# Reordering the second tile's attention, interleaving the first groups of the first product, and splitting the last rows of a fused attention and feed-forward kernel

## The chip, the cores, the metric

One core of one Trainium2 chip. The metric is the device time of one execution in microseconds (us). A program on one core has no second die to compare with, so a run counts as slow when it is over 1.5% above the fastest of its kernel; every run told of here is of the state fast. Ratios are the mean time of one kernel's fast runs over the mean of the other's fast runs of the same rounds, so they are not quite the ratio of the medians that I quote beside them.

## The reference, cut to what matters

```python
def _attn_ref(q, k, v):              # (8, 8, 576, 64) each; nine chunks of 64 rows
    scores = scale * np.matmul(q_c, k_c.transpose(0, 1, 2, 4, 3))
    scores = scores - np.max(scores, axis=-1, keepdims=True)
    attn = np.exp(scores)
    attn = attn / (np.sum(attn, axis=-1, keepdims=True) + 1e-09)
    return np.matmul(attn, v_c)      # back to (8, 8, 576, 64)

def _moe_ref(x, w_in, w_out):        # (4608, 512), (512, 2048), (2048, 512)
    h = x @ w_in
    g = 0.5 * h * (1.0 + erf(h * inv_sqrt2))
    return g @ w_out
```

## The kernel before

The 4608 tokens are cut into nine tiles of 512. A tile goes through attention (four pairs of heads, `g`), a first product `mm1` (16 groups of four matmuls, each followed by a GELU on ACT) and a second product `mm2` (16 slots of four matmuls). The attention of tile t+1 is placed between the slots of tile t's second product. The first two tiles differ from the later ones: weights are still arriving and being cast, and q and k are transposed on PE instead of by the transfers.

Names in what follows: PE multiplies matrices, ACT is ScalarE, DVE VectorE, POOL GpSimd, and SP (SyncE) issues transfers. In the attention the scores go into `s_ps`, their exponentials into `pT`, the sums of these into `sums_ps`, the reciprocals, spread over the tile, into `rc` (by way of `rb`), the product with v into `av_ps`, and the result is `x`. To evacuate is to copy a finished result out of PSUM, so that its buffer comes free.

```python
    def att_sums(t):

        sum_ps = ps_at.tile([P, MT], f32, tag="at", name="sums_ps")
        for g in range(G):
            nc.tensor.matmul(sum_ps[QD * g:QD * (g + 1)], ones_c[:], tiles[t]["pT", g][:], start=True, stop=True,
                             tile_position=(0, QD * g))
        t1 = work.tile([P, NB, 32], f32, tag="t1", name="t1", bufs=2)
        nc.vector.transpose(t1[:], sum_ps[:].rearrange("p (n e) -> p n e", e=32))
        r1 = work.tile([P, 2, NB], f32, tag="r1", name="r1", bufs=2)
        nc.vector.reciprocal(r1[:], t1[:].rearrange("p n (r e) -> p r n e", r=2)[:, :, :, 0])
        rb = work.tile([P, G, NB], f32, tag="rb", name="rb", bufs=2)
        for g in range(G):
            for s in range(G):
                nc.scalar.copy(rb[QD * s:QD * (s + 1), g], r1[QD * g:QD * (g + 1), s // 2])
        tiles[t]["rb"] = rb

    def att_rc(t, g):

        rb = tiles[t]["rb"]
        rc = work.tile([P, NB, 32], f32, tag="rc", name="rc", bufs=4)
        nc.vector.transpose(rc[:], rb[:, g].to_broadcast([P, NB, 32]))
        tiles[t]["rc", g] = rc
...
    def att_av(t, g):
        st = tiles[t]
        av_ps = ps_at.tile([P, CT, CH], f32, tag="at", name="av_ps")
        for i in range(CT):
            nc.tensor.matmul(av_ps[:, i, :], v_bds[t % NV][:, i, g, :], st["pT", g][:, i, :], start=True, stop=True)
        nc.vector.tensor_tensor(
            st["x"][:, g, :], av_ps[:].rearrange("p i e -> p (i e)"),
            st["rc", g][:].rearrange("p n e -> p (n e)"), op=mybir.AluOpType.mult)

    NB = MT // 32
    DV, AC, PO = nc.vector.tensor_copy, nc.scalar.copy, nc.gpsimd.tensor_copy

    def att_units(t, cq=DV, ck=DV):
        tiles[t]["x"] = xpool.tile([P, G, MT], bf16, tag="x", name="x")
        T = []
        for g in range(G):
            T += [lambda g=g: att_Tq(t, g, cq), lambda g=g: att_Tk(t, g, ck)]
        S_ = [lambda g=g: att_S(t, g) for g in range(G)]
        if t > 1:
            T = [lambda g=g: flip_k(t, g, ck) for g in range(G)]
            S_ = [lambda g=g: att_S_flipped(t, g) for g in range(G)]
            U = [lambda: att_sums(t), *[lambda g=g: att_rc(t, g) for g in range(G)]]
        else:
            U = [lambda g=g: att_sum(t, g) for g in range(G)]
        A = [lambda g=g: att_av(t, g) for g in range(G)]
        return T, S_, U, A


    def mm1_slot(t, f):
        st = tiles[t]
        if f == 0:
            st["h"] = hpool.tile([P, FF, MT], bf16, tag="h", name="h")
        h_ps = ps_mm.tile([P, MT], f32, tag="mm", name="h_ps")
        for ks in range(KS):
            nc.tensor.matmul(h_ps[:], w_in_sb[:, ks, f * P:(f + 1) * P], st["x"][:, ks, :],
                             start=(ks == 0), stop=(ks == KS - 1))
        nc.scalar.activation(st["h"][:, f, :], h_ps[:], Act.Gelu)

    NQ = 4
    def mm2_slot(t, ms, qt):
        st = tiles[t]
        if qt == 0:
            pool, tag = (ps_at, "at") if t == 0 and ms == 3 else (ps_mm, "mm")
            st["y_ps", ms] = pool.tile([P, d_model], f32, tag=tag, name="y_ps")
        y_ps = st["y_ps", ms]
        for f in range(qt * FF // NQ, (qt + 1) * FF // NQ):
            nc.tensor.matmul(y_ps[:], st["h"][:, f, ms * P:(ms + 1) * P], w_out_sb[:, f, :],
                             start=(f == 0), stop=(f == FF - 1))
        if qt == NQ - 1:
            y_sb = ypool.tile([P, d_model], f32, tag="y", name="y_sb")
            (AC if t == 0 or ms % 2 == 0 and t + 1 < NT else DV)(y_sb[:], y_ps[:])
            if t < B:
                m0 = t * S + ms * P
                nc.sync.dma_start(out[m0:m0 + P, :], y_sb[:])
            else:
                for c in range(P // CH):
                    m0 = (ms * (P // CH) + c) * S + MT
                    nc.sync.dma_start(out[m0:m0 + CH, :], y_sb[c * CH:(c + 1) * CH, :])

    def phase(t, extra1, extra2, halved=False):
        nms = MT // P
        if halved:
            order = [(ms, qt) for ms in range(nms) for qt in (0, 1)]
            order += [(ms, qt) for qt in (2, 3) for ms in range(nms)]
        else:
            order = [(ms, qt) for ms in range(nms) for qt in range(NQ)]
        for f in range(FF):
            for u in extra1.get(f, ()):
                u()
            mm1_slot(t, f)
        for s, (ms, qt) in enumerate(order):
            for u in extra2.get(s, ()):
                u()
            mm2_slot(t, ms, qt)
        for u in extra2.get("end", ()):
            u()
...
        for g in range(G):
            cast_v(1, 0, PO, slice(g, g + 1))

        T, S_, U, A = att_units(1, DV, AC)
        def next_qk():
            for nm in "qk":
                load_qk(2, nm)
        phase(0, {}, {5: T[0:2], 6: T[2:4], 7: [*T[4:6], S_[0]], 8: [*T[6:8], S_[1]],
                      9: [U[0], S_[2]], 10: [U[1], next_qk], 11: [S_[3], U[2]],
                      
                      12: [lambda: act_table(Act.Gelu), *[lambda g=g: cast_v(1, 1, AC, slice(g, g + 1)) for g in range(G)]],
                      13: [U[3]], 14: [A[0]], 15: [A[1]], "end": [A[2], A[3]]}, halved=True)
        pool_cast_qk(2)
```

`ps_mm` has three PSUM buffers (h_ps and y_ps share them), `ps_at` three (scores, sums, av; one of them is held by y3 during tile 0's second product), `ps_tp` two.

The softmax here doesn't subtract the row's maximum and nothing guards it: scores larger than these inputs give would overflow.

Of the kernel before, what the change touches and what calls it, by code (L numbers as in the profile page):

```python
# [11 lines left out]
def kernel(  # L12
# [9 lines left out]
    nc = tc.nc  # L22
    P = 128
    f32 = mybir.dt.float32
    bf16 = mybir.dt.bfloat16
    Act = mybir.ActivationFunctionType

    B, H, S, D = q.shape
    CH = 64
# [3 lines left out]
    G = H // 2  # L33
# [99 lines left out]
    def cast_v(t, r, copy, gs=slice(0, G)):  # L133
        sl = slice(CH * r, CH * (r + 1))
        copy(v_bds[t % NV][sl, :, gs, sl].rearrange("p i g d -> p g i d"), tiles[t]["vf"][sl, gs])  # L135
# [9 lines left out]
    def att_Tq(t, g, copy):  # L145
        tp = transposed(t, "q", g)
        qT = work.tile([P, CT, CH], bf16, tag="qT", name="qT", bufs=5)
        copy(qT[:].rearrange("p i (c j) -> p i c j", j=J), tp)
        tiles[t]["qT", g] = qT

    def att_Tk(t, g, copy):
        tp = transposed(t, "k", g)
        for r in range(2):
            sl = slice(CH * r, CH * (r + 1))
            copy(k_bds[g][sl, :, sl].rearrange("p i (c j) -> p i c j", j=J), tp[sl])  # L155
# [16 lines left out]
    def att_S_flipped(t, g):  # L172

        st = tiles[t]
        s_ps = ps_at.tile([P, CT, CH], f32, tag="at", name="s_ps")
        qt = st["qt"][:, g * J:(g + 1) * J].rearrange("p j (i c) -> p i j c", i=CT)
        for i in range(CT):
            nc.tensor.matmul(s_ps[:, i, :].rearrange("p (j c) -> p j c", j=J), k_bds[g][:, i, :], qt[:, i],  # L178
                             start=True, stop=True)
        pT = work.tile([P, CT, CH], bf16, tag="pT", name="pT", bufs=5)  # L180
        nc.scalar.activation(pT[:].rearrange("p i (c j) -> p i c j", j=J),  # L181
                             s_ps[:].rearrange("p i (j c) -> p i c j", j=J), Act.Exp, scale=scale)
        st["pT", g] = pT

    def att_S(t, g):
        st = tiles[t]
        s_ps = ps_at.tile([P, CT, CH], f32, tag="at", name="s_ps")
        for i in range(CT):
            nc.tensor.matmul(s_ps[:, i, :], k_bds[g][:, i, :], st["qT", g][:, i], start=True, stop=True)  # L189
        pT = work.tile([P, CT, CH], bf16, tag="pT", name="pT", bufs=5)  # L190
        nc.scalar.activation(pT[:], s_ps[:], Act.Exp, scale=scale)  # L191
        st["pT", g] = pT
# [34 lines left out]
# [6 lines that stand above are left out]
# [35 lines left out]
    def att_units(t, cq=DV, ck=DV):  # L268
        tiles[t]["x"] = xpool.tile([P, G, MT], bf16, tag="x", name="x")
        T = []  # L270
        for g in range(G):
            T += [lambda g=g: att_Tq(t, g, cq), lambda g=g: att_Tk(t, g, ck)]
        S_ = [lambda g=g: att_S(t, g) for g in range(G)]
        if t > 1:
            T = [lambda g=g: flip_k(t, g, ck) for g in range(G)]
            S_ = [lambda g=g: att_S_flipped(t, g) for g in range(G)]
            U = [lambda: att_sums(t), *[lambda g=g: att_rc(t, g) for g in range(G)]]
        else:
            U = [lambda g=g: att_sum(t, g) for g in range(G)]
        A = [lambda g=g: att_av(t, g) for g in range(G)]  # L280
        return T, S_, U, A


    def mm1_slot(t, f):
        st = tiles[t]
        if f == 0:
            st["h"] = hpool.tile([P, FF, MT], bf16, tag="h", name="h")
        h_ps = ps_mm.tile([P, MT], f32, tag="mm", name="h_ps")
        for ks in range(KS):
            nc.tensor.matmul(h_ps[:], w_in_sb[:, ks, f * P:(f + 1) * P], st["x"][:, ks, :],  # L290
                             start=(ks == 0), stop=(ks == KS - 1))
        nc.scalar.activation(st["h"][:, f, :], h_ps[:], Act.Gelu)  # L292

    NQ = 4
    def mm2_slot(t, ms, qt):
        st = tiles[t]
        if qt == 0:
            pool, tag = (ps_at, "at") if t == 0 and ms == 3 else (ps_mm, "mm")
            st["y_ps", ms] = pool.tile([P, d_model], f32, tag=tag, name="y_ps")
# [12 lines that stand above are left out]
                    m0 = (ms * (P // CH) + c) * S + MT  # L312
                    nc.sync.dma_start(out[m0:m0 + CH, :], y_sb[c * CH:(c + 1) * CH, :])

    def phase(t, extra1, extra2, halved=False):
        nms = MT // P
        if halved:
            order = [(ms, qt) for ms in range(nms) for qt in (0, 1)]
            order += [(ms, qt) for qt in (2, 3) for ms in range(nms)]
        else:  # L320
            order = [(ms, qt) for ms in range(nms) for qt in range(NQ)]
        for f in range(FF):
            for u in extra1.get(f, ()):
                u()
            mm1_slot(t, f)
# [6 lines that stand above are left out]
# [40 lines left out]
    def act_table(func):  # L372
        nc.scalar.activation(act_scratch[:], rest[:, 0:1], func)  # L373

    with tc.manual_schedule():
# [74 lines left out]
                wout[c](i, PO)  # L450
        for g in range(G):
            cast_v(1, 0, PO, slice(g, g + 1))

        T, S_, U, A = att_units(1, DV, AC)
        def next_qk():
            for nm in "qk":
                load_qk(2, nm)
        phase(0, {}, {5: T[0:2], 6: T[2:4], 7: [*T[4:6], S_[0]], 8: [*T[6:8], S_[1]],
                      9: [U[0], S_[2]], 10: [U[1], next_qk], 11: [S_[3], U[2]],
                      
                      12: [lambda: act_table(Act.Gelu), *[lambda g=g: cast_v(1, 1, AC, slice(g, g + 1)) for g in range(G)]],
                      13: [U[3]], 14: [A[0]], 15: [A[1]], "end": [A[2], A[3]]}, halved=True)
        pool_cast_qk(2)
        for t in range(1, NT):
            nxt = t + 1 < NT
# [46 lines left out]
```

## Time and profile before

| | before |
|---|---|
| median of the first three runs | 299.74 us (299.62 to 300.56) |
| span of the profiled run | 297.1 us |
| PE busy | 283.0 us, 95% |
| tile 0's second product | 21.21 us, where 17.8 would do |
| last matmul's end to the end of the span | 5.0 us |

The busy share of PE says that the kernel is near its bound, not where the rest lies. For that one compares stages that do the same work in different tiles, and then asks for the waits inside the stage that is too long. The lines are in the prediction.

### The profile page before, as it was taken

The page shows a single profiled execution, that of the slowest core. Times are in us where ns is not written, and L with a number is a line of the kernel's source. Part 1 is how long each engine was busy: PE and PEld are TensorE (multiplying, and loading weights), DVE is VectorE, ACT ScalarE, POOL GpSimd, SP SyncE. Part 2 cuts the span into 40 slices and gives each one's busy share as a digit, 9 for nine tenths or more (in the row PEclk, how much of TensorE's full clock was granted, in tenths as well). Part 3 has the DMA queues.
Part 4 walks back from the last instruction along what each step waited for, and adds up shares of the span by engine and source line. Part 5 has one row for each costly group of instructions (what it writes and reads, how often), then busy time and mean ns, then how long its engine had stood idle before and what let it go on. Part 6 is the DMA issues. An engine that isn't in the chain of part 4 may idle for free.

```text
span 297.1 us, 4797 instructions
## 1 busy us (share of the span) xinstructions
PE 283.0 (95%) x1820; PEld 138.4 (47%) x1855; DVE 125.4 (42%) x207; ACT 176.1 (59%) x366; POOL 95.3 (32%) x134
## 2 busy tenths in 40 slices
PE   6799988999999999999999999999999999999993
PEld 2554454444544554455445444544454445444441
DVE  6775258441826072517250735163146341630020
ACT  3746377777636863686368637863687368636400
POOL 7869655407620640083006500650002700000000
PEclk9999999999999999999999999999999999999999
DMA  6999999799749814981499149804999850020033
GB/s 225 271 370 407 393 279 305 206 216 308 210 134 283 220 69 131 294 218 54 134 276 238 50 138 291 236 37 135 194 126 149 235 121 2 35 106 2 0 71 71
DMA packets 96198, 53.78 MB, mean 181 GB/s; under 512 B 68528, under 2 KB 87984, under 8 KB 96176
## 3 DMA queue, kind: packets, MB, share of 16 engines
q1 hardware_dynamic: 96176, 53.49, 66.3%
q8 instruction: 14, 0.23, 0.3%
q14 instruction: 8, 0.07, 0.1%
HBM read 36.70 MB, written 9.44 MB: 155 GB/s over the span
## 4 chain that ended last, share of the span: by engine, by line
PE 92%; DVE 3%; ACT 2%; issue 2%; ACTq 0%
PE h_ps L290 41%; PE y_ps L302 41%; PE av_ps L260 3%; PE s_ps L178 2%; ACT k_bd L155 2%; PE tp L142 1%; PE s_ps L189 1%; PE sums_ps L215 1%; PE sum_ps L197 1%; PE rc_ps L248 1%; DVE x L261 1%; DVE t L201 0%; ACT pT L191 0%; DVE q_nat L131 0%; DVE v_bd L73 0%
## 5 line engine op out<-in xcount | busy, mean ns | idle before, releaser
L302 PE MATMUL y_ps<-w_out_sb,h 128*128 128x512 bf16 x554 | 133.6, 379 | 1.1
L290 PE MATMUL h_ps<-x,w_in_sb 128*128 128x512 bf16 x564 | 125.8, 379 | 1.2 <-DVE x L261 0.4
L292 ACT ACTIVATE h<-h_ps 128x512 bf16<-128x512 f32 x144 | 86.0, 597 | 63.5 <-PE h_ps L290 63.5
L290 PEld LDWEIGHTS <-w_in_sb 128*128 128x128 bf16 x576 | 56.1, 98 | 68.8 <-issue 1.7
L302 PEld LDWEIGHTS <-h 128*128 128x128 bf16 x576 | 51.5, 98 | 53.0 <-issue 1.6
L170 DVE COPY k_bd<-k_t 64x512 bf16<-64x512 bf16 x56 | 34.2, 611 | 48.8 <-DMA k_t<-k_nat 47.6
L131 POOL CAST q_nat<-arrival 128x512 bf16<-128x512 f32 x32 | 19.7, 655 | 99.9 <-DMA arrival<-in_q_dram 96.4
L135 POOL CAST v_bd<-arrival 64x2048 bf16<-64x2048 f32 (+1 forms) x26 | 33.8, 1306 | 20.8 <-DMA arrival<-in_v_dram 12.8
L224 ACT COPY rb<-r 32x16 f32<-32x16 f32 x112 | 22.6, 202 | 14.1 <-DVE r L220 12.6
L306 DVE COPY y_sb<-y_ps 128x512 f32<-128x512 f32 x18 | 12.4, 688 | 39.6 <-PE y_ps L302 39.6
L261 DVE TENSOR_TENSOR x<-av_ps,rc 128x512 bf16<-128x512 f32 x36 | 24.5, 689 | 4.0 <-PE av_ps L260 1.1
L218 DVE STREAM_TRANSPOSE t<-sums_ps 128x512 f32<-128x512 f32 x7 | 5.0, 717 | 48.7 <-PE sums_ps L215 48.7
L131 POOL CAST k_nat<-arrival 128x512 bf16<-128x512 f32 x32 | 18.6, 618 | 12.2 <-DMA arrival<-in_k_dram 6.8
L373 ACT ACT_TABLE_LOAD x17 | 21.8, 1283 | 1.0 <-PEq L496 0.7
L231 DVE STREAM_TRANSPOSE rc<-rb 128x512 f32<-128x512 f32 x28 | 19.7, 704 | 6.4 <-ACT rb L224 6.4
L260 PEld LDWEIGHTS <-v_bd 128*128 128x128 bf16 x288 | 13.0, 99 | 7.9 <-issue 0.4
L306 ACT COPY y_sb<-y_ps 128x512 f32<-128x512 f32 x18 | 10.3, 589 | 8.4 <-PE y_ps L302 8.4
L155 ACT COPY k_bd<-tp 64x512 bf16<-64x512 bf16 x16 | 9.3, 579 | 9.3 <-PE tp L142 9.1
L181 ACT ACTIVATE pT<-s_ps 128x512 bf16<-128x512 f32 x28 | 14.7, 592 | 0.0
L260 PE MATMUL av_ps<-pT,v_bd 128*128 128x64 bf16 x288 | 14.3, 194 | 0.1
L178 PEld LDWEIGHTS <-k_bd 128*128 128x128 bf16 x224 | 10.4, 98 | 6.6
L178 PE MATMUL s_ps<-q_t,k_bd 128*128 128x64 bf16 x224 | 11.1, 193 | 0.0
(55 smaller groups left out, 105.7 us busy)
## 6 DMA issues: line engine op xcount, KB each, us to landing
arrival<-in_v_dram SPq DMA_DIRECT2D x72, 128.0 KB, 4.2
out_dram<-y_sb SPq DMA_DIRECT2D x32, 256.0 KB, 2.0
arrival<-in_q_dram SPq DMA_DIRECT2D x7, 1024.0 KB, 6.2
arrival<-in_k_dram SPq DMA_DIRECT2D x7, 1024.0 KB, 8.8
arrival<-in_moe_w_out_dram SPq DMA_DIRECT2D x4, 1024.0 KB, 13.3
arrival<-in_moe_w_in_dram SPq DMA_DIRECT2D x3, 1024.0 KB, 10.5
arrival<-in_q_dram SPq DMA_DIRECT2D x4, 256.0 KB, 4.2
arrival<-in_k_dram SPq DMA_DIRECT2D x4, 256.0 KB, 4.5
```

Source lines behind the costliest of these rows:

```text
L131: copy(st[nm][:, g].rearrange("p j r d -> p r j d"), st[nm + "f"][:, 2 * g:2 * g + 2])
L135: copy(v_bds[t % NV][sl, :, gs, sl].rearrange("p i g d -> p g i d"), tiles[t]["vf"][sl, gs])
L170: copy(k_bds[g][sl, :, sl].rearrange("p i (c j) -> p i c j", j=J), src[sl])
L178: nc.tensor.matmul(s_ps[:, i, :].rearrange("p (j c) -> p j c", j=J), k_bds[g][:, i, :], qt[:, i], start=True, stop=True)
L224: nc.scalar.copy(rb[QD * s:QD * (s + 1), g], r1[QD * g:QD * (g + 1), s // 2])
L260: nc.tensor.matmul(av_ps[:, i, :], v_bds[t % NV][:, i, g, :], st["pT", g][:, i, :], start=True, stop=True)
L261: nc.vector.tensor_tensor(st["x"][:, g, :], av_ps[:].rearrange("p i e -> p (i e)"), st["rc", g][:].rearrange("p n e -> p (n e)"), op=mybir ...
L290: nc.tensor.matmul(h_ps[:], w_in_sb[:, ks, f * P:(f + 1) * P], st["x"][:, ks, :], start=(ks == 0), stop=(ks == KS - 1))
L292: nc.scalar.activation(st["h"][:, f, :], h_ps[:], Act.Gelu)
L302: nc.tensor.matmul(y_ps[:], st["h"][:, f, ms * P:(ms + 1) * P], w_out_sb[:, f, :], start=(f == 0), stop=(f == FF - 1))
L306: (AC if t == 0 or ms % 2 == 0 and t + 1 < NT else DV)(y_sb[:], y_ps[:])
L373: nc.scalar.activation(act_scratch[:], rest[:, 0:1], func)
```

## The change

Its intent: fill PE where tile 1's attention leaves it waiting. q is transposed first and copied by ACT, k's copies are shared between ACT and DVE, the sums of the four head pairs are made by four column-tiled matmuls (each fills a quarter of the rows of one PSUM buffer) as in the later tiles. The first mm1 groups of tiles 0 and 1 run slice by slice of K, so that PE has work while the last x is made. The last 128 rows are cut into two column halves, so that half of the evacuation and transfer lies beside matmuls.

```diff
-        s_ps = ps_at.tile([P, CT, CH], f32, tag="at", name="s_ps")
+        pool, tag = (ps_tp, "tp") if t == 1 and g > 1 else (ps_at, "at")
+        s_ps = pool.tile([P, CT, CH], f32, tag=tag, name="s_ps")
...
-            T += [lambda g=g: att_Tq(t, g, cq), lambda g=g: att_Tk(t, g, ck)]
+            T += [lambda g=g: att_Tq(t, g, cq), lambda g=g: att_Tk(t, g, ck if t == 0 or g % 2 == 0 else DV)]
...
+        if t > 0:
             U = [lambda: att_sums(t), *[lambda g=g: att_rc(t, g) for g in range(G)]]
...
-    def mm1_slot(t, f):
+    def mm1_slot(t, f, n=1):
...
+        h_ps = [ps_mm.tile([P, MT], f32, tag="mm", name="h_ps") for _ in range(n)]
         for ks in range(KS):
+            for a in range(n):
+                nc.tensor.matmul(h_ps[a][:], w_in_sb[:, ks, (f + a) * P:(f + a + 1) * P], st["x"][:, ks, :],
+                                 start=(ks == 0), stop=(ks == KS - 1))
+        for a in range(n):
+            nc.scalar.activation(st["h"][:, f + a, :], h_ps[a][:], Act.Gelu)
...
+    def last_rows(t, ms):
+        h = d_model // 2
+        for a, (pool, tag) in enumerate(((ps_mm, "mm"), (ps_at, "at"))):
...
+            (AC if a == 0 else DV)(y_sb[:], y_ps[:])
+            for c in range(P // CH):
+                m0 = (ms * (P // CH) + c) * S + MT
+                (nc.sync if c == 0 else nc.scalar).dma_start(
+                    out[m0:m0 + CH, a * h:(a + 1) * h], y_sb[c * CH:(c + 1) * CH, :])
...
+        first = (2, 3, 1)[min(t, 2)]
+        mm1_slot(t, 0, first)
+        for f in range(first, FF):
...
+            cast_v(1, 1, PO, slice(g, g + 1))
...
-        T, S_, U, A = att_units(1, DV, AC)
+        T, S_, U, A = att_units(1, AC, AC)
...
+        phase(0, {}, {0: [lambda: act_table(Act.Exp)],
+                      3: [T[0]], 4: [T[2]], 5: [T[4]], 6: [T[6], T[1]], 7: [T[3]], 8: [T[5], S_[0]], 9: [T[7], S_[1], next_qk],
+                      10: [S_[2], S_[3]], 11: [U[0], lambda: act_table(Act.Gelu)], 12: [U[1], A[0]], 13: [U[2], A[1]],
+                      14: [U[3], A[2]], 15: [U[4], A[3]]}, halved=True)
```

Two things are easily overlooked. The second half of tile 1's v casts, `cast_v(1, 1, ...)`, moves from ACT to POOL. And the scores of tile 1's third and fourth pair of heads take their PSUM buffers from `ps_tp`, not from `ps_at`; no run tested that alone.

More of the change, by code (lines that the diff above doesn't have):

```diff
@@ L287, in mm1_slot @@
             st["h"] = hpool.tile([P, FF, MT], bf16, tag="h", name="h")
-        h_ps = ps_mm.tile([P, MT], f32, tag="mm", name="h_ps")
+        h_ps = [ps_mm.tile([P, MT], f32, tag="mm", name="h_ps") for _ in range(n)]
         for ks in range(KS):
-            nc.tensor.matmul(h_ps[:], w_in_sb[:, ks, f * P:(f + 1) * P], st["x"][:, ks, :],
-                             start=(ks == 0), stop=(ks == KS - 1))
-        nc.scalar.activation(st["h"][:, f, :], h_ps[:], Act.Gelu)
+            for a in range(n):
[3 more added lines that the diff above has]
+            nc.scalar.activation(st["h"][:, f + a, :], h_ps[a][:], Act.Gelu)
     NQ = 4
@@ L296, in mm2_slot @@
         st = tiles[t]
+        if t == NT - 1 and ms == MT // P - 1:
+            if qt == 0:
+                last_rows(t, ms)
+            return
         if qt == 0:
@@ L313, in mm2_slot @@
                     nc.sync.dma_start(out[m0:m0 + CH, :], y_sb[c * CH:(c + 1) * CH, :])
+    def last_rows(t, ms):
+        h = d_model // 2
+        for a, (pool, tag) in enumerate(((ps_mm, "mm"), (ps_at, "at"))):
+            y_ps = pool.tile([P, h], f32, tag=tag, name="y_ps")
+            for f in range(FF):
+                nc.tensor.matmul(y_ps[:], tiles[t]["h"][:, f, ms * P:(ms + 1) * P],
+                                 w_out_sb[:, f, a * h:(a + 1) * h], start=(f == 0), stop=(f == FF - 1))
+            y_sb = ypool.tile([P, h], f32, tag="y", name="y_sb")
+            (AC if a == 0 else DV)(y_sb[:], y_ps[:])
[3 more added lines that the diff above has]
+                    out[m0:m0 + CH, a * h:(a + 1) * h], y_sb[c * CH:(c + 1) * CH, :])
     def phase(t, extra1, extra2, halved=False):
@@ L321, in phase @@
             order = [(ms, qt) for ms in range(nms) for qt in range(NQ)]
-        for f in range(FF):
+        first = (2, 3, 1)[min(t, 2)]
+        mm1_slot(t, 0, first)
+        for f in range(first, FF):
             for u in extra1.get(f, ()):
@@ L457, in next_qk @@
                 load_qk(2, nm)
-        phase(0, {}, {5: T[0:2], 6: T[2:4], 7: [*T[4:6], S_[0]], 8: [*T[6:8], S_[1]],
-                      9: [U[0], S_[2]], 10: [U[1], next_qk], 11: [S_[3], U[2]],
-                      12: [lambda: act_table(Act.Gelu), *[lambda g=g: cast_v(1, 1, AC, slice(g, g + 1)) for g in range(G)]],
-                      13: [U[3]], 14: [A[0]], 15: [A[1]], "end": [A[2], A[3]]}, halved=True)
+        phase(0, {}, {0: [lambda: act_table(Act.Exp)],
+                      3: [T[0]], 4: [T[2]], 5: [T[4]], 6: [T[6], T[1]], 7: [T[3]], 8: [T[5], S_[0]], 9: [T[7], S_[1], next_qk],
+                      10: [S_[2], S_[3]], 11: [U[0], lambda: act_table(Act.Gelu)], 12: [U[1], A[0]], 13: [U[2], A[1]],
+                      14: [U[3], A[2]], 15: [U[4], A[3]]}, halved=True)
         pool_cast_qk(2)
```

## The prediction

> **What bounds the kernel now.** I read the page first (busy shares, slices, chain), then the stretches of single stages, then PE's waits, then the order of time around the second tile and the end. From the page:
>
> ```profile
> PE 283.0 (95%) x1820; PEld 138.4 (47%) x1855; DVE 125.4 (42%) x207; ACT 176.1 (59%) x366; POOL 95.3 (32%) x134
> ...
> PE   6799988999999999999999999999999999999993
> ...
> PE 92%; DVE 3%; ACT 2%; issue 2%; ACTq 0%
> ```
>
> PE is full nearly everywhere, and 92% of the chain that ended last is PE's. PE's matmul work is not cut by this change (but for the sums), so all that can be won is PE's idle time: slices 1 and 2 (start), the dip at slices 6 and 7 (37 to 52 us), and the end. To size the dip I compare stages. Columns: the stretch, its length, then busy time of the engines.
>
> ```profile
> 18.50:32.91 14.41, 14.03 (x69) 6.27 (x68) 8.28 (x13) 10.02 (x17) 11.36 (x12) 1.00 1.06 398
> 32.91:54.12 21.21, 19.10 (x162) 10.29 (x164) 11.88 (x23) 13.64 (x23) 11.64 (x22) 1.00 0.90 290
> 54.12:68.60 14.48, 14.09 (x70) 6.24 (x68) 6.05 (x10) 9.80 (x17) 3.02 (x5) 1.00 0.94 230
> 68.60:84.70 16.10, 15.94 (x130) 8.15 (x132) 7.00 (x11) 9.97 (x27) 11.41 (x12) 1.00 0.77 236
> 84.70:98.50 13.80, 13.75 (x64) 6.23 (x64) 5.48 (x9) 8.96 (x15) 1.93 (x4) 1.00 0.92 256
> ```
>
> An undisturbed first product (mm1: 64 matmuls of 512 columns) takes 13.80 us (84.70 on), 0.216 us a matmul. Tile 0's takes 14.41 (0.61 too long), tile 1's 14.48 (0.68 too long). The undisturbed second product with the next tile's attention takes 16.10; the one at 32.91 also has 8 groups of 4 transposes, 0.22 each, so it should take 17.8, and takes 21.21: 3.4 too long. What it waited for (total, times, longest), PE's waits from 30 to 56 us:
>
> ```profile
> PE s_ps L189 <- DVE t L201: 0.8, 1, 0.8
> PE tp L142 <- ACT k_bd L155: 0.7, 2, 0.5
> PE sum_ps L197 <- ACT pT L191: 0.4, 1, 0.4
> PE h_ps L290 <- DVE x L261: 0.2, 1, 0.2
> ```
>
> After 62 us PE waits for nothing at all. So 0.6 + 3.4 + 0.7 = 4.7 us, plus the end, is all there is to win: 1.6% plus a little.
>
> **The Trainium skill.** "TensorE: Matmul & The Clock Gate", Back-to-back issue gap: N/2.4 + 2.5 ns warm, so 216 ns for 512 columns; the trace agrees (13.80/64 = 0.2156). By it 256 columns take 109 ns (an estimate), so cutting 16 matmuls into 32 halves is 3.5 us against 3.45: free, if the extra weight loads hide; here 8 matmuls of 64 columns with their loads take 0.23 us, so they hide. "ScalarE: Activation LUTs", What ACT_TABLE_LOAD costs: 1283 ns plus a drain of 1380 for each switch; here the load is 1.28 us and the next activation follows at once, so I use 1.28 + 0.20. "DMA: Bandwidth & Descriptors", Issuing engines are not separate DMA queues: a second issuing engine saves only the sequencer's time to issue; here an issue is 0.58 us, and at the end two lie one behind the other. Its "Anatomy of one DMA" gives about 2 us fixed; the last output transfers land after 2.2 to 2.4.
>
> **Part 1, tile 0's first two mm1 groups K-slice by K-slice.** Now PE does three matmuls from 18.50 and stands for the last x slice until 19.75 (1.25 us for 0.65 of work). With two groups interleaved it has six (1.29 us) until 19.79, when slice 4 is there. Both groups end at 20.22, now 19.75 + 0.22 + 0.86 = 20.83. Gain 0.6. The first GELU starts no later than now, a third mm buffer is free, and the casts of the weights for groups 2 and 3 end at 20.0 and 18.2. So the second product starts at M = 32.3 instead of 32.91.
>
> **Part 2, tile 1's attention.** I follow it from M, slots of four y matmuls being 0.86. The instruction order of the changed program is read from its build. ACT finishes GELU at M+0.8, loads the Exp table till M+2.3, copies qT0 from M+3.1; three q transposes with a slot between each are free of waits, as two tp buffers and copies of 0.6 keep up. k81 is copied by ACT M+6.9 to 8.1 (two of 0.59), k82 by DVE M+7.6 to 9.0 (two of about 0.69, the qT copy's time), k83 by ACT 8.7 to 9.9, k84 by DVE 10.0 to 11.3. The exps stand on ACT behind k83: 9.9 to 11.0 for two. S2 goes at 10.8; S3 stands 0.3 for k84 and starts at 11.4; pT3 ends at M+12.45. The sums therefore start at B = M+12.5 with almost no further wait. The four column-tiled sums take 0.33 us of PE instead of 4 x 0.216 = 0.86: gain 0.5 of PE work. The av groups need v, whose casts POOL now all does: 44.93 + 8 x 0.57 = 49.5, at two a head; this just keeps pace (46.1, 47.2, 48.4, 49.5).
>
> What comes after the sums is read from the third tile, which already does it this way:
>
> ```profile
> 73.94 0.40 PE L215 MATMUL sums_ps<-pT,ones_c 128*32 128x512 bf16 x4
> ...
> 74.44 0.72 DVE L218 STREAM_TRANSPOSE t<-sums_ps 128x512 f32<-128x512 f32 x1 [6.46 <-PE sums_ps L215]
> ...
> 75.19 0.35 DVE L220 RECIPROCAL r<-t 128x32 f32<-128x32 f32 x1
> ...
> 75.58 3.44 ACT L224 COPY rb<-r 32x16 f32<-32x16 f32 x16 [1.77 <-DVE r L220]
> ...
> 76.46 0.71 DVE L231 STREAM_TRANSPOSE rc<-rb 128x512 f32<-128x512 f32 x1 [0.91 <-ACT rb L224]
> ...
> 77.28 0.69 DVE L261 TENSOR_TENSOR x<-av_ps,rc 128x512 bf16<-128x512 f32 x1
> 77.88 0.70 DVE L231 STREAM_TRANSPOSE rc<-rb 128x512 f32<-128x512 f32 x1
> ...
> 79.04 1.28 ACT L373 ACT_TABLE_LOAD   x1
> ```
>
> From the start of the sums: DVE finishes x0 after 4.03 and one more head every 1.42 (rc 0.6, x 0.8): x at B + 4.0, 5.5, 6.9, 8.3 = M+16.5, 18.0, 19.4, 20.8. ACT is done with the sixteen rb copies at B+5.1, with the Gelu table at B+6.6 = M+19.1, and only then evacuates y0 to y3: done at M+19.7, 20.2, 20.7, 21.2 (four took 2.05 us at 52.90). PE meanwhile: y3 holds one of three at-buffers, so av2 must wait for x0 and av3 for x1; slot 15 ends at M+19.1. The first three mm1 groups then need the buffers of y0, y1 and y2, given up at M+19.7, 20.2 and 20.7: their first matmuls are paced by ACT, the other nine follow (1.94) and end at M+22.9. Group 3 needs group 0's buffer, whose GELU ends about 0.4 later, at M+23.3 = 55.6. In the kernel before, group 3 starts at 55.43 + 0.22 + 2 x 0.86 = 57.4. Gain at this place: 1.75 us, of which 0.6 is part 1's; so tile 1 itself gives only about 1.1 of its 4.1 us of loss. The wait that was transposes and sums becomes a wait for ACT's small copies, table load and evacuations.
>
> **Part 3, the last 128 rows.** Views: order of time at the end, and the output transfers.
>
> ```profile
> 285.93 8.01 SPq L313 DMA_DIRECT2D out_dram<-y_sb  x6
> ...
> 292.12 0.69 DVE L306 COPY y_sb<-y_ps 128x512 f32<-128x512 f32 x1 [2.71 <-PE y_ps L302]
> ...
> DMA to landing us min/median/max: 2.2/2.4/2.4
> ```
>
> Today: the evacuation of 0.69, two issues one after the other (292.83 and 293.40), 2.4 to land, and 1.3 to the span's end at 297.1. Changed: the first column half is evacuated and sent under the second's matmuls. The second's evacuation has 256 columns; 0.69 less 256 x 1.04 ns (an estimate: one column a cycle of 0.96 GHz, the rate that leaves 0.15 of fixed cost) is 0.42: gain 0.27. The two issues go side by side on SP and ACT: gain 0.57. Half the bytes: 0.05. Sum 0.9.
>
> **Sum.** 1.75 + 0.9 = 2.65. 299.74 - 2.65 = 297.1 us, 0.9% less.
>
> **Rivals.** (a) ACT's tail does not bind, for instance because rb copies, table and evacuations fall while PE is busy: then mm1 starts at M+18.1 and group 3 at about M+21: 4 us at this place, 4.9 in all, 294.8. For it: the third tile does the same chain without a wait of PE. Against: there 7 slots of y follow the last av, here one, and y leaves early there. (b) The exps come later than I count, as ACT now does qT, half of k, exps and rb: each us later of B moves everything one for one, and at 1.5 later only parts 1 and 3 are left: 298.3. For it: ACT's work before the sums is 7.5 us between M+3 and M+12.5. (c) The gain is given back at tile 2, whose transfers keep their times. k's copies end at 67.99 and the last S is at 71.89; v is ready at 71.70 and the first av is at 75.14. Slack 3.4 or more against a shift of 1.8: kept. It would bind only in (a). (d) The first transfer issued by ACT costs more than SP's: at most some tenths lost from part 3.
>
> **Range and chances.** (a) in part gives 296.0, (b) in part 298.4; that is my range. 2% is 6.0 us, and 4.7 plus 0.9 is less than that even if every loss vanished. So faster by 2% has 0.02; slower by 2% would need a stall of 6 us that nothing shows, 0.01.
>
> **What would show it.** Right: mm1's first two groups of tile 0 without a gap, and the second product near 32.3; PE's waits on k_bd and t gone, new ones of h_ps on ACT's y_sb (and av on x) near 51 to 53; group 3 of tile 1 at 55.6; no PE wait after 60; at the end an evacuation of 0.4, and two issues at once. Wrong: tile 1's mm1 starting before 51.5 (a), sums starting after 46 (b), a wait of PE on k_bd or v_bd after 66 (c), or a last transfer landing later than 2.6 after its issue (d).

## The result, and the profile after

The changed kernel takes 296.63 us (median of 4, 295.75 to 297.31) against 299.68 (299.03 to 300.56): ratio 0.9895, 95% interval 0.9857 to 0.9932. Run again on another chip with more rounds it is 296.58 (6 runs) against 299.75, ratio 0.9891 (0.9866 to 0.9916). That is 3.2 us off; 297.1 was predicted, and the measured time is inside the range.

The same three stages as before (busy times of stretches of the changed kernel; start, length, then the engines):

```profile
17.79:31.95 14.16, 13.89 (x62) 6.27 (x65) 9.43 (x13) 9.60 (x17) 11.43 (x13) 1.00 1.05 398
31.95:52.02 20.07, 19.02 (x163) 9.58 (x165) 9.98 (x18) 14.20 (x35) 13.53 (x24) 1.00 0.99 312
52.02:66.78 14.76, 14.23 (x63) 6.25 (x64) 5.83 (x10) 10.15 (x18) 4.15 (x8) 1.00 0.89 231
```

They were 14.41, 21.21 and 14.48 us, and are 14.16, 20.07 and 14.76. So tile 0's mm1 gained 0.25, its second product with tile 1's attention 1.1, and tile 1's mm1 lost 0.3. PE's waits of the changed kernel from 30 to 57 us:

```profile
PE av_ps L261 <- POOL v_bd L135: 0.3, 1, 0.3
PE h_ps L293 <- ACT h L296: 0.3, 1, 0.3
PE h_ps L293 <- ACT y_sb L314: 0.2, 1, 0.2
PE s_ps L190 <- DVE k_bd L155: 0.2, 1, 0.2
```

The waits of the transposes on ACT's copies, those on the exps and on the sums' transposition are gone, as is the wait on x; 0.2 us for one of DVE's copies of k is left, and v, the evacuations of y and a GELU are new. After 57 us the same view is empty, as it was. On the page, the chain that ended last was 92% PE's; now it is 81% PE's, with 7% DMA, 4% SP's queue and 3% POOL, so transfers and their casts have come in. The order of time of the changed kernel shows what came in between:

```profile
42.95 2.29 POOL L381 CAST w_out_sb<-arrival 128x512 bf16<-128x512 f32 x4 [1.42 <-DMA arrival<-in_moe_w_out_dram]
...
45.19 5.32 POOL L135 CAST v_bd<-arrival 64x512 bf16<-64x512 f32 x8
...
46.54 3.44 ACT L225 COPY rb<-r 32x16 f32<-32x16 f32 x16 [1.83 <-DVE r L221]
...
49.99 1.28 ACT L397 ACT_TABLE_LOAD   x1
...
50.56 0.41 PE L261 MATMUL av_ps<-pT,v_bd 128*128 128x64 bf16 x8
...
51.40 2.03 ACT L314 COPY y_sb<-y_ps 128x512 f32<-128x512 f32 x4
...
52.02 3.29 PE L293 MATMUL h_ps<-x,w_in_sb 128*128 128x512 bf16 x12 [0.19 <-ACT y_sb L314]
...
55.56 0.81 PE L293 MATMUL h_ps<-x,w_in_sb 128*128 128x512 bf16 x3 [0.25 <-ACT h L296]
```

Follow it from the top. POOL stands 1.42 us for the last quarter of w_out, casts it, and then casts v in eight pieces until 50.51. The last av starts at 50.56, 0.05 after. Meanwhile ACT goes through the small rb copies, the table load and the evacuations of y; mm1 stands for the first of these until 52.02. Then group 3 stands until 55.56 for the GELU of group 0. So in this trace ACT holds mm1 last, but not by much: where nothing of ACT's holds it (a3, a4, b1, b3, c1 and c4 below), mm1 starts 1.11 us after the start of the last av, which would be 51.67 here.

The end of the changed kernel, in the order of time: the two issuing engines and the last evacuation.

```profile
289.00 2.27 SPq L334 DMA_DIRECT2D out_dram<-y_sb  x2
289.00 2.30 ACTq L334 DMA_DIRECT2D out_dram<-y_sb  x2
290.35 0.43 DVE L331 COPY y_sb<-y_ps 128x256 f32<-128x256 f32 x1 [2.75 <-PE y_ps L328]
```

Each engine issues two transfers (the first of each pair at 289.00, under the second half's matmuls, the second at 290.8), where SP issued two in a row after the last evacuation. That evacuation is 0.43 us instead of 0.69.

One thing in these two traces is not the change. Here is one line, the same 16 matmuls of tile 0's attention, from the order of time of the kernel before:

```profile
15.62 1.81 PE L248 MATMUL rc_ps<-ident_f,rr 128*64 128x128 f32 x16 [0.35 <-DVE rr L242]
```

and of the changed kernel:

```profile
15.31 1.09 PE L249 MATMUL rc_ps<-ident_f,rr 128*64 128x128 f32 x16 [0.28 <-DVE rr L243]
```

The code is the same, yet 1.81 us became 1.09 (1.54 and 0.82 between first and last start). The Trainium skill, "TensorE: Matmul & The Clock Gate", What's actually happening, says that PE starts at half its clock and is released after a busy window of about 3.4 us that runs freely and does not start with the kernel. The traces agree that the point moves: in 7 of the 14 traces of this study the 16 matmuls start within 0.82 us (PE is fast), in the other 7 within 1.40 to 1.56. It is not always one late release, though: in b1 and c4 eight score matmuls just before had taken 0.41 us, where they take 0.61 in the trace of the kernel before, and PE was slow again in the 16. Of the four traces with the old start of tile 0 two are of each sort, of the ten with the new one five are, so it is not the change. Together with the arrival of the first transfers it spreads the start of mm1 over 2.3 us (17.3 to 19.6). Totals of kernels that differ by a few tenths say little for this reason; below I also give lengths of stages.

### The profile page after: what moved, and what is told of

It is laid out like the page before. It is cut to its first block, busy times and chain, and to the rows that moved or that the text cites. A ratio compares the mean times of both kernels' runs of the same rounds, so it can differ in the third digit from the quotient of the medians.

```text
span 294.0 us, 4846 instructions
## 1 busy us (share of the span) xinstructions
PE 281.9 (96%) x1837; PEld 138.2 (47%) x1871; DVE 126.5 (43%) x201; ACT 177.1 (60%) x380; POOL 98.6 (34%) x138
## 4 chain that ended last, share of the span: by engine, by line
PE 81%; DMA 7%; SPq 4%; POOL 3%; ACT 2%; issue 1%; DVE 1%
PE h_ps L293 37%; PE y_ps L310 37%; DMA arrival<-in_moe_w_out_dram 4%; DMA arrival<-in_moe_w_in_dram 3%; PE av_ps L261 2%; PE s_ps L178 2%; SPq L127 2%; SPq L112 1%; PE y_ps L328 1%; ACT rb L225 1%; POOL w_in_sb L373 1%; PE sums_ps L216 1%; POOL w_out_sb L381 1%; POOL v_bd L462 1%; ACT y_sb L314 0%
## 5 line engine op out<-in xcount | busy, mean ns | idle before, releaser
L310 PE MATMUL y_ps<-w_out_sb,h 128*128 128x512 bf16 x539 | 130.5, 379 | 1.0
L310 PEld LDWEIGHTS <-h 128*128 128x128 bf16 x560 | 49.6, 98 | 50.0 <-issue 1.8
L170 DVE COPY k_bd<-k_t 64x512 bf16<-64x512 bf16 x56 | 35.6, 635 | 48.0 <-DMA k_t<-k_nat 47.0
L131 POOL CAST q_nat<-arrival 128x512 bf16<-128x512 f32 x32 | 20.9, 692 | 95.2 <-DMA arrival<-in_q_dram 69.0
L135 POOL CAST v_bd<-arrival 64x512 bf16<-64x512 f32 (+1 forms) x30 | 36.5, 1216 | 20.3 <-DMA arrival<-in_v_dram 11.4
L225 ACT COPY rb<-r 32x16 f32<-32x16 f32 x128 | 25.8, 202 | 16.2 <-DVE r L221 14.5
L314 DVE COPY y_sb<-y_ps 128x512 f32<-128x512 f32 x17 | 11.7, 687 | 36.9 <-PE y_ps L310 36.9
L219 DVE STREAM_TRANSPOSE t<-sums_ps 128x512 f32<-128x512 f32 x8 | 5.7, 718 | 50.3 <-PE sums_ps L216 50.3
L232 DVE STREAM_TRANSPOSE rc<-rb 128x512 f32<-128x512 f32 x32 | 22.5, 704 | 7.3 <-ACT rb L225 7.3
L131 POOL CAST k_nat<-arrival 128x512 bf16<-128x512 f32 x32 | 18.6, 618 | 11.6 <-DMA arrival<-in_k_dram 5.7
L261 PEld LDWEIGHTS <-v_bd 128*128 128x128 bf16 x288 | 12.8, 98 | 9.5 <-POOL v_bd L135 2.5
L155 ACT COPY k_bd<-tp 64x512 bf16<-64x512 bf16 x12 | 6.9, 579 | 4.8 <-PE tp L142 4.7
## 6 DMA issues: line engine op xcount, KB each, us to landing
arrival<-in_moe_w_out_dram SPq DMA_DIRECT2D x4, 1024.0 KB, 12.8
```

Source lines behind the costliest of these rows:

```text
L131: copy(st[nm][:, g].rearrange("p j r d -> p r j d"), st[nm + "f"][:, 2 * g:2 * g + 2])
L135: copy(v_bds[t % NV][sl, :, gs, sl].rearrange("p i g d -> p g i d"), tiles[t]["vf"][sl, gs])
L170: copy(k_bds[g][sl, :, sl].rearrange("p i (c j) -> p i c j", j=J), src[sl])
```

## The experiments

Each kernel was timed in five rounds beside the kernel before on the same chip; all results are correct. "mm1(1)" is the first product of tile 1, "S" the first score matmul after it. The columns are from the order of time of each run's one profile, in us.

| run | median (runs) | ratio to before, 95% | start of tile 0's second product | start of mm1(1) | its length | last matmul to end |
|---|---|---|---|---|---|---|
| before | 299.68 (4) | | 32.91 | 54.12 | 14.47 | 4.98 |
| change, first profile | 296.63 (4) | 0.9895 | 31.95 | 52.02 | 14.77 | 3.66 |
| a1_tail | 298.26 (6) | 0.9969 (0.9945 to 0.9994) | 33.37 | 54.81 | 14.47 | 3.98 |
| a2_slices0 | 299.32 (6) | 0.9992 (0.9971 to 1.0013) | 33.25 | 55.12 | 14.47 | 4.97 |
| a3_tile1 | 297.39 (6) | 0.9932 (0.9913 to 0.9951) | 31.82 | 53.33 | 13.81 | 4.67 |
| a4_tile1_slices | 297.54 (6) | 0.9932 (0.9912 to 0.9952) | 32.79 | 52.92 | 14.70 | 4.65 |
| b0_after | 296.58 (6) | 0.9891 (0.9866 to 0.9916) | 31.56 | 52.38 | 14.77 | 3.66 |
| b1_table | 296.71 (6) | 0.9891 (0.9863 to 0.9919) | 33.45 | 54.04 | 14.23 | 3.66 |
| b2_headsums | 297.40 (6) | 0.9921 (0.9900 to 0.9942) | 31.81 | 53.53 | 14.23 | 3.67 |
| b3_two | 295.90 (4) | 0.9872 (0.9850 to 0.9895) | 33.26 | 53.45 | 13.81 | 3.67 |
| c1_one | 296.54 (5) | 0.9896 (0.9876 to 0.9917) | 32.68 | 53.58 | 13.81 | 3.65 |
| c2_two_v | 296.22 (5) | 0.9888 (0.9868 to 0.9907) | 33.28 | 53.06 | 14.11 | 3.68 |
| c3_two_table_v | 296.12 (5) | 0.9885 (0.9865 to 0.9905) | 33.40 | 52.93 | 14.64 | 3.65 |
| c4_two_vdouble | 297.56 (6) | 0.9931 (0.9901 to 0.9962) | 32.85 | 53.11 | 13.81 | 3.69 |

From S to the end of the last matmul all 14 traces take 223.48 to 223.53 us: nothing is won or given back there.

### The parts one by one

**a1_tail**, the kernel before with only the new end:

```diff
-        if qt == 0:
+        if t == NT - 1 and ms == MT // P - 1:
+            if qt == 0:
+                last_rows(t, ms)
+            return
```

> The kernel before with only the last 128 rows in two column halves. From the traces of the two kernels the end of the last matmul to the end of the span is 4.96 us before and 3.67 after. Theory: the part alone gives that 1.3 us (evacuation 0.26, issue side by side 0.57, earlier landing and end 0.4), and nothing else moves: 298.4 if before is 299.7. Rival: the split end is worth only the 0.9 of the prediction, and the other 0.4 is chance of one run: then last matmul to end is about 4.0. Either way the first 290 us are as before.

The ratio is 0.9969, 0.9 us; from the last matmul to the end it takes 3.98 us instead of 4.98. That is the rival's figure and the prediction's, not the 1.3 that I had read from the pair of traces. The other 0.3 shows up where I did not look for it: a3 and a4, with the old end, take 4.67 and 4.65. In those kernels, as in all with tile 1's change, the closing sequence after the last transfer is 0.3 shorter; why is open, since its code was not touched.

**a2_slices0**, the kernel before with `first = (2, 1, 1)`.

> The kernel before with only tile 0's first two mm1 groups run K-slice by K-slice. Prediction: mm1 of tile 0 takes 13.8 instead of 14.41 us, 0.6 off the total. What the trace of the whole change shows: 14.16, because PE then waits for the weights' cast of the second group, so 0.25 to 0.6 off. Rival: the stretch shrinks but the start of mm1 itself moves by up to 0.7 from run to run, as PE's slow first stretch (0.61 us instead of 0.40 for the same matmul) ends at 17.3 in one trace and at 13.4 in the other; then totals tell little, and only the stretch from the first mm1 matmul to the first y matmul does.

0.9992, 0.2 us, and the interval holds zero. Tile 0's mm1 took 14.68 us in this profile, no less than before. PE's waits of this run have the reason:

```profile
PE h_ps L293 <- DVE w_in_sb L373: 0.7, 1, 0.7
```

Interleaving removes the wait for x, and 3.6 us later, at 22.2, PE stands 0.7 us for the cast of a weight block that has only just arrived. In b1, b3, c1, c2 and c4, where mm1 starts at 18.9 or later, the weights are there and the stretch takes 13.81, the full 0.6 less; in a2 it started at 18.6 and the weights were late as well, and so in c3, the longest with 15.07 (from 18.33, with waits of 0.17 and 0.73 us for such casts). The gain hangs on which of two arrivals is first.

**a3_tile1** (tile 1's attention alone, `first = (1, 1, 1)`, old end) and **a4_tile1_slices** (the same with `first = (1, 3, 1)`).

> The kernel before with only tile 1's attention reordered (q early, k on two engines, column-tiled sums), all mm1 groups one by one, old end. Theory that ACT's evacuations and DVE's x pace the start of tile 1's mm1: group 0 has to wait for x of the last head (about 21.2 us after the second product starts), groups 1 to 3 follow at full speed, so group 3 starts at about 23.2 us after the second product's start, against 24.46 before: 1.2 off the total. Rival (PE's own work sets it): group 3 starts 20.7 to 21 us after, 3.5 off.

> As the run with tile 1's attention alone, and tile 1's first three mm1 groups K-slice by K-slice. Intent of the change: PE has nine matmuls to fill the wait for the last x, so this should be faster than one by one. Theory: it is not, since three groups need three buffers that ACT gives up one after the other, and group 3 then waits for the GELU of group 0 (0.4): group 3 starts 23.6 us after the second product, as in the changed kernel, 0.4 later than one by one. So 0.8 off the kernel before.

Both have 0.9932, 2.0 us: more than either expectation of mine, less than the rival's 3.5. From the start of tile 0's second product group 3 starts 24.10 us after in a3 and 23.62 in a4 (from the order of time: 55.92 less 31.82, 56.41 less 32.79); the first should have been 23.2. The length of mm1(1) behaves as I had said: one by one it is 13.81, undisturbed; interleaved by three it is 14.70, and PE's waits of a4 from 50 to 58 us name the GELU:

```profile
PE h_ps L293 <- ACT h L296: 0.3, 1, 0.3
```

But the start of mm1(1), 53.33 in a3, was later after the second product's start than I had reckoned, and not for x. That was the clue for the next runs. The parts add up: 0.31 + 0.08 + 0.68 = 1.07%, and the whole gives 1.09%.

### What paces the start of tile 1's mm1

**b0_after** is the changed kernel again.

> The changed kernel again, to be compared with the three that follow on the same chip. Expected 2.6 to 3.1 us under the kernel before; its profile tells whether PE's slow first stretch ends early (as in its first trace) by chance: if it ends near 17 here, the start of mm1 is at 18.5 as before and that 0.7 is not the change's.

The gain holds, 0.9891. PE was fast early again in its profile (mm1 from 17.33), and yet the second product's start to S took 35.58 us against 34.83 in the first trace of the same code: the early start was lost again on the way. So something fixed in time lies in between. PE's waits of this run show one such thing:

```profile
PE tp L142 <- POOL q_nat L131: 0.5, 1, 0.5
```

The first transposition of tile 1's q stood for POOL's cast of it, which began at 34.37, when the transfer of q had landed. a3, the other trace in which mm1 starts before 17.5, has the same wait of 0.5. The next runs look for what follows.

**b1_table**, the changed kernel with the Gelu table loaded later:

```diff
-                      10: [S_[2], S_[3]], 11: [U[0], lambda: act_table(Act.Gelu)], 12: [U[1], A[0]], 13: [U[2], A[1]],
-                      14: [U[3], A[2]], 15: [U[4], A[3]]}, halved=True)
+                      10: [S_[2], S_[3]], 11: [U[0]], 12: [U[1], A[0]], 13: [U[2], A[1]],
+                      14: [U[3], A[2]], 15: [U[4], A[3]], "end": [lambda: act_table(Act.Gelu)]}, halved=True)
```

> The changed kernel with the load of the Gelu table in tile 0's second product moved behind the four evacuations of y. Theory that ACT's tail (rb copies, table, evacuations) sets the start of tile 1's mm1: the buffers come free 1.5 us earlier, mm1 starts when slot 15 ends (0.1 earlier than now, as av waits for v and x), but nine matmuls no longer stand for buffers, and group 3 starts about 0.6 earlier, 0.6 off the total. Rival: DVE's chain of rc and x alone sets it (last x at 53.2 in the trace): then the first mm1 matmul hardly moves and group 3 moves by under 0.2.

No difference: 0.9891 both. The order of time of this run shows why:

```profile
47.58 5.30 POOL L135 CAST v_bd<-arrival 64x512 bf16<-64x512 f32 x8
...
51.22 1.07 ACT L314 COPY y_sb<-y_ps 128x512 f32<-128x512 f32 x2
...
52.93 0.41 PE L261 MATMUL av_ps<-pT,v_bd 128*128 128x64 bf16 x8
...
54.04 2.75 PE L293 MATMUL h_ps<-x,w_in_sb 128*128 128x512 bf16 x12
```

ACT begins to evacuate y right after the rb copies, at 51.22, with time to spare, and mm1 does not start before 54.04: POOL's casts of v end at 52.88, the last av starts at 52.93, one slot of y follows, then mm1. So the theory that ACT alone paces this stage fell. The new one: POOL's chain of casts, released by the transfer of the last quarter of w_out, sets the last av and with it the earliest start of mm1(1). From POOL's first cast of that quarter to the last av it is 7.61 us in the first trace of the changed kernel (50.56 less 42.95) and 7.58 to 7.61 in a3, a4, b0, b1, b3 and c1, though the transfer itself comes anywhere from 42.95 to 45.35. mm1(1) goes with it: it starts 8.69 to 8.79 us after that first cast in a3, a4, b0, b1, b3 and c1 (9.07 in the first trace, where ACT holds it), while counted from the second product's start it is anywhere from 20.07 to 21.51. The transfer in turn hangs on POOL: in the first trace of the changed kernel SP, which issues it, stood 4.5 us before the third quarter and 0.6 before the last until POOL's casts of earlier quarters had given back staging buffers, and the last quarter landed at 42.90.

**b2_headsums**, the changed kernel with tile 1's sums head by head (`if t > 1` for `if t > 0`, and no fifth unit).

> The changed kernel with tile 1's sums head by head, as in the kernel before (one matmul of 512 columns, transposition, reciprocal and transposition a head), rest as changed. If column tiling is worth its intent, this is slower: PE does 0.53 us more. Theory: ACT is freed of sixteen copies (3.4 us), so the evacuations end earlier, while DVE does 4 x 1.7 instead of 1.1 + 4 x 0.7; the last x comes at about the same time, and group 3 starts 0.3 to 0.8 earlier: equal or faster by up to 0.8.

Slower than the changed kernel, 0.9921 against 0.9891 (297.40 against 296.58 at the median), so the column-tiled sums earn their place; my expectation had the wrong sign. PE's waits:

```profile
PE av_ps L261 <- DVE x L262: 1.6, 2, 0.8
```

The sums of each head take one of the two PSUM buffers that the first two scores, the sums and av share, and av stands for x to give one back. I had counted busy time and forgotten buffers.

**b3_two**, the changed kernel with `first = (2, 2, 1)`.

> The changed kernel with two instead of three of tile 1's first mm1 groups interleaved. Theory: the third group has a buffer of its own, group 3 need not stand for group 0's GELU, and only two evacuations pace the start: group 3 starts about 0.8 earlier. Rival (three groups fill the wait for x better): it starts 0.2 or more later.

295.90 and 0.9872, the best ratio of all. The stretch of tile 1's mm1 in this run:

```profile
53.45:67.26 13.81, 13.81 (x65) 6.27 (x64) 5.00 (x9) 9.86 (x18) 4.00 (x8) 1.00 0.99 245
```

It takes 13.81, with no wait, and group 3 starts 22.78 us after the second product, against 23.61 in the first trace of the changed kernel: the 0.8 that was expected. The third group has a buffer of its own and no GELU to wait for. In the same call the changed kernel has 0.9891; the intervals overlap, so 0.5 us of gain is likely but not shown by the times. What is shown is that mm1(1) itself became 0.96 us shorter.

**c1_one**, the changed kernel with `first = (2, 1, 1)`.

> The changed kernel with tile 1's mm1 groups one by one (tile 0's first two interleaved as changed, new end kept). Theory now: in the changed kernel the last av of tile 1 follows POOL's last v cast by 0.05 us in every trace, and those casts follow the last quarter of w_out, so mm1 of tile 1 starts about 8.7 us after POOL's first cast of that quarter whatever the order of groups; x of the last head is there within 0.7 of that. One by one needs one y buffer at the start and no wait for GELU: from the start of mm1 to group 3 2.6 us (changed kernel: 3.5), as with two interleaved. Expected 0.5 to 0.8 under the changed kernel, the same as two interleaved within 0.3. Rival (interleaving is what fills the wait for x): slower than the changed kernel by 0.4.

The stretch is 13.81 here too, and mm1(1) starts 8.69 us after POOL's first cast, both as expected, but the time is 296.54 (0.9896), within the noise of the changed kernel's. Neither the gain of 0.5 nor the rival's loss of 0.4 can be read from it.

**c4_two_vdouble**, a control: two interleaved groups, and head 0's v cast twice by POOL.

```diff
         for g in range(G):
-            cast_v(1, 0, PO, slice(g, g + 1))
-            cast_v(1, 1, PO, slice(g, g + 1))
+            for _ in range(2 if g == 0 else 1):
+                cast_v(1, 0, PO, slice(g, g + 1))
+                cast_v(1, 1, PO, slice(g, g + 1))
```

> Control: two interleaved groups, all v casts on POOL, and head 0's two casts done twice (same values), 1.3 us more on POOL ahead of the others. Theory that POOL's casts pace tile 1: the last av and the second product of tile 1 come 1.3 later with respect to the last quarter of w_out, and the kernel is 1.0 to 1.4 slower than with two interleaved. Rival (ACT's evacuations or DVE's x bind): under 0.4 slower.

297.56, ratio 0.9931 against 0.9872 for b3, so 1.7 us slower (the two were timed on different chips, each beside the kernel before). Against c1, timed beside it and also without a wait in mm1(1), it is 1.0 us slower, with intervals that just overlap; so the size in time is rough, and the lengths have to carry the argument. First the order of time of b3, then of c4:

```profile
44.73 2.30 POOL L381 CAST w_out_sb<-arrival 128x512 bf16<-128x512 f32 x4 [2.20 <-DMA arrival<-in_moe_w_out_dram]
...
46.97 5.32 POOL L135 CAST v_bd<-arrival 64x512 bf16<-64x512 f32 x8
...
52.34 0.41 PE L261 MATMUL av_ps<-pT,v_bd 128*128 128x64 bf16 x8
```

```profile
43.07 2.29 POOL L381 CAST w_out_sb<-arrival 128x512 bf16<-128x512 f32 x4 [1.51 <-DMA arrival<-in_moe_w_out_dram]
...
45.30 6.64 POOL L135 CAST v_bd<-arrival 64x512 bf16<-64x512 f32 x10
...
52.00 0.41 PE L261 MATMUL av_ps<-pT,v_bd 128*128 128x64 bf16 x8
```

From POOL's first cast of the last quarter to the last av: 7.61 us in b3, 8.93 in c4. The difference, 1.32, is the 1.32 that POOL's casts of v got longer (5.32 to 6.64). PE's last av follows POOL's last cast by 0.05 in both, and mm1(1) starts 10.04 us after the first cast instead of 8.72, later by 1.32. So all of the added work came through, and none of it was slack. This is the test that the theory could have failed. (c4's profiled run happens to be one of its two fast ones, 295.92, with the transfer early at 43.07; the other four are 297.39 to 298.90.)

**c2_two_v** and **c3_two_table_v**: two interleaved groups, head 0's v cast by DVE, and for c3 also the later table.

```diff
         for g in range(G):
-            cast_v(1, 0, PO, slice(g, g + 1))
-            cast_v(1, 1, PO, slice(g, g + 1))
+            if g:
+                cast_v(1, 0, PO, slice(g, g + 1))
+                cast_v(1, 1, PO, slice(g, g + 1))
...
-                      10: [S_[2], S_[3]],
+                      10: [S_[2], S_[3], lambda: cast_v(1, 0, DV, slice(0, 1)), lambda: cast_v(1, 1, DV, slice(0, 1))],
```

> Two interleaved groups, and the casts of head 0's v put on DVE (which waits for the sums just then), six left on POOL. Theory that POOL's casts pace av: the last cast and the last av come 1.3 earlier with respect to the last quarter of w_out, but the evacuations of y on ACT then bind, as mm1's buffer is free only 2.0 after the last rb copy: mm1 of tile 1 starts about 0.4 earlier, so 0.3 to 0.5 faster than two interleaved alone. Rival (POOL's pacing is chance, PE or DVE's x binds): no change, or slower where DVE's two casts delay the sums' transposition.

> As the run before it, and the Gelu table loaded behind the evacuations. With POOL relieved the moved load, which did nothing alone, should now count: mm1 starts when PE's slot 15 ends, and the last x (about 8.3 after the sums) becomes the bound: a further 0.2 to 0.5. The best of all versions, about 295.3. Rival: no gain over two interleaved with v moved, as x binds already.

0.9888 and 0.9885: no gain over b3 (0.9872, on another chip), and none clear of noise over c1 (0.9896, timed beside them). The forecast of the lengths missed too. Counted from POOL's first cast of the last quarter, the last av comes after 7.50 us in c2 and 7.11 in c3, against 7.61 in b3: 0.1 and 0.5 earlier, not 1.3. mm1(1) starts after 9.13 and 8.20 us, against 8.72. (From the second product's start it is 19.78 and 19.53 against 20.19, but in c2 that is no gain of the edit: its transfer had come 0.8 earlier than b3's.) POOL did end earlier, 6.6 us after its first cast instead of 7.6; what came next took over. In c2 mm1(1) stands 0.4 us for ACT's evacuation, as the theory said of ACT, and av stands 0.7 for x. In c3, with the table out of the way, what is won at the start is lost inside. PE's waits of c3:

```profile
PE h_ps L293 <- DVE x L262: 0.7, 1, 0.7
PE av_ps L261 <- DVE x L262: 0.6, 2, 0.5
```

With POOL and the table out of the way the bound is DVE's x: av stands for buffers that x must give back, and the last K slice of mm1 stands 0.7 us for x, so mm1(1) takes 14.64. Three chains, POOL's, ACT's and DVE's, end close together here (the waits that appear when one is relieved are 0.4 to 0.7 us), and relieving one only shows the next. In c3 x of the third head came 0.4 us later after x of the second than in b3 (53.59 less 51.79, against 52.78 less 51.37), and in c2 as well; the profile puts that on DVE's own preceding instruction; I did not find out why.

## Why the prediction was right

**Bound and ceiling.** Right. All the gain lies in the start, tile 1 and the end; from S on nothing changed, 223.48 and 223.53 us. So "faster by 2%" was out of reach, as reckoned.

**Part 1, tile 0's groups: 0.6.** Mis-sized. The wait for x went, but a wait for the cast of weights took its place in the runs where mm1 starts early; alone it measured 0.2 us with an interval that holds zero, and 0.25 in the first trace.

**Part 2, tile 1.** The times came out well: group 3 predicted at 55.6, measured at 55.56; mm1 predicted to stand for y's buffers at M+19.7 = 52.0, measured 52.02; a GELU wait after it, measured 0.25. A part of that is luck: the second product started at M = 31.95 and not 32.3, and counted from it the two are 20.07 and 23.61, each 0.3 to 0.4 later than reckoned. The mechanism that I named, ACT's tail, is what held mm1(1) in both traces of the changed kernel, by 0.35 us in the first and by 0.1 in b0. The step that failed is "this just keeps pace", on POOL's casts of v, which I priced at 0.57 us each. They take 0.66 (5.32 for eight), they begin with the arrival of the last quarter of w_out, and they, not PE or ACT, set the last av: 7.6 us after that arrival in seven traces; the exceptions are b2, where buffers bind, the control, and the two that moved casts to DVE. Where that transfer is later, or ACT's tail shorter, POOL's casts hold mm1(1); the prediction took their start, 44.93, from the trace of the kernel before and left its spread out of the account. Tile 1 alone measured 2.0 us instead of 1.1. Of the surplus 0.3 is in the shorter closing sequence. Some of the rest may be that tile 1 is now tied to a transfer and absorbs a late start: with mm1 of tile 0 starting at 18.9 to 19.6, S comes at 66.9 to 68.3, and with a start at 17.3 to 17.9 it comes at 66.8 to 67.8. That compares different kernels, so it is a suggestion, not a finding; the remainder is open.

**Part 3, the end: 0.9.** Right: 0.93 alone, by time, and 1.0 in its trace. The evacuation's estimate of 0.42 measured 0.43. Its 1.04 ns a column was taken from no trace; the two sizes now measured give 1.02 (0.69 less 0.43, over 256 columns). The issues lie side by side, and the 32 half matmuls cost PE the 0.05 us of the estimate (223.53 us from S to the last matmul with the new end, 223.48 to 223.49 with the old).

**Rivals.** (a), PE free of ACT's tail: no, mm1 started at 52.0, not before 51.5. (b), exps late: the sums started at 44.87, M+12.9 by the trace's own M, 0.4 later than reckoned, so only a trace of it. (c), given back at tile 2: no wait of PE after 57. (d), a dear issue on ACT: 0.50 to 0.56 us against SP's 0.47, nothing.

So the total, 2.65 predicted and 3.2 measured, is right within the range, with part 1 over-priced by 0.4 and part 2 under-priced by 0.9. That the sum is nearer than its parts is luck.

## What to carry to other kernels

Where a stage waits, list every engine's chain into the next stage with its end, not just the one that binds: here POOL's, ACT's and DVE's ended so close that no single relief tried (table, v, sums) made the kernel faster, and a control that lengthened one chain said more than those that shortened it. Interleaving more groups than there are spare buffers trades a wait for data for a wait for buffers: two groups with three buffers ran without a gap, three lost 0.9 to 1.0 us (0.4 where the table was moved). And when a start-up state moves by chance, compare lengths of stages from the traces, and let timed runs decide only what is larger than their spread.

## What the Trainium skill lacked or had wrong

- "TensorE: Matmul & The Clock Gate", What you observe, gives the release of PE's clock a spread of ±500 ns from run to run. That is said of matmuls without a break; in this start-up, where PE pauses, the change to fast came at 13.4 us in the changed kernel's first trace and at about 17 in the kernel before, and in b1 and c4 PE was fast from 12.8 and 12.2 and slow again by 16.1 and 15.5. So for a start-up with pauses 500 ns is too little.
- The same page, Back-to-back issue gap, gives a sustained 131 ns for a pair of weight load and matmul of 512 columns, beside 216 ns for the isolated gap. Here 64 such pairs in a row take 13.81 us, 216 ns each.
- "ScalarE: Activation LUTs", What ACT_TABLE_LOAD costs, adds a drain of 1380 ns to the load of 1283. Here the load takes 1.28 us, starts at 49.99 when the copy before it ends at 49.98, and the next activation starts at 51.29: no drain shows.
- No page says what makes the stretch from the last transfer's landing to the end of the span longer or shorter (the nearest is "Runtime: NRT & Kernel Launch", The ~15µs preamble/postamble breakdown). Here it took 1.29 to 1.35 us in the kernels without tile 1's change and 0.97 to 1.03 in those with it.
